# Two interleaved attention layers: the norm's statistics on ScalarE in two passes, its small steps on GpSimd, the pad in a tile of its own, and orders searched for it

## The chip, the cores and the metric

The kernel runs on one core of a Trainium2 chip. The metric is the device time of one execution in microseconds (us), taken as the median of several runs. A profiled execution of the same program gives the trace from which all other times here come. Engines are named as in the profile: PE is TensorE (matmul), PEld its weight load, DVE is VectorE, ACT is ScalarE, POOL is GpSimd, and SP is the engine whose queue starts the DMA transfers.

## What is computed

Four layers over 2048 tokens of width 512, each a residual around a norm and an attention of 32 heads of width 16. Layers 0 and 2 (type A) let each token attend to 8 tokens, 2 apart; layers 1 and 3 (type B) to the last 256 tokens. All numbers are float32 in and out.

```python
def _layernorm(x, axis=-1, eps=1e-5):
    m = jnp.mean(x, axis=axis, keepdims=True)
    v = jnp.var(x, axis=axis, keepdims=True)
    return (x - m) / jnp.sqrt(v + eps)
...
    x = A_x
    x = x + _A_ref(_layernorm(x, axis=-1), A_wqkv, A_wo)
    x = x + _B_ref(_layernorm(x, axis=-1), B_wqkv, B_wo)
    x = x + _A_ref(_layernorm(x, axis=-1), A_wqkv, A_wo)
    x = x + _B_ref(_layernorm(x, axis=-1), B_wqkv, B_wo)
    return x
```

## The kernel before, in words

The tokens are cut into 8 chunks of 256 (`C`), a chunk into two halves of 128 (`t` = 0, 1). For each chunk `layer_a` and then `layer_b` are recorded; layers 0 and 1 go over all chunks, then layers 2 and 3. That gives 32 norms, 16 ahead of A layers and 16 ahead of B layers.

**The norm** (`norm`, from L921). For each half DVE takes `bn_stats` (L936, 128x512) and `bn_aggr` (L939), which leave mean and variance in `mv`. Then come three small steps on 128x2 for both halves at once: `spread_` (L942, DVE) adds eps and scales, `rstd` (L945, POOL) raises to the power -1/2, `shift` (L948, DVE) multiplies the negative mean by that. With these two columns in `rs`, ACT normalises each half in one pass (L964 or L986). In a B layer, PE then transposes the result (L990), ACT copies it out as float16 high parts (L995) and DVE makes the low parts (L996); in an A layer a DMA transposes both parts. Projections (L1015 to L1017, and L1035 to L1038) follow on PE.

**An A layer.** DVE multiplies keys and queries (L1152), PE sums over heads (L1160), DVE and ACT make the softmax of 8 weights, PE spreads the weights (L1229), DVE weighs the values (L1242), and POOL (or DVE, L1247) sums them in three additions (L1249 to L1251).

**A B layer.** Queries and keys go through DRAM into the stacked tiles `stk` (L1286, L1297). A first pass of scores on PE (L1339, L1342) gives the maximum of each row on DVE: for most chunks a masked pick (L1361) and a reduction (L1357); in the first chunk of each B layer, which has no chunk before it, one instruction that adds a mask and takes the maximum (L1353). That instruction also writes its whole sum out, though only the maximum is used: the output goes to `junk`, a tile that nobody reads. The maxima join the stacked tiles as two more rows, so a second pass of scores (L1433, L1435) comes out with the maximum taken off; ACT takes the exponential (L1439), POOL sets the masked triangle to zero (L1448), and PE multiplies by the values (L1465).

**The residual** (`finish`). ACT (L1059) and POOL or DVE (L1061) split the attention's output into high and low parts, PE projects, and DVE adds the residual (L1069) into the tile `y` (or `x`), which the next norm reads.

**The pad.** Rows 48 to 63 and 112 to 127 of `stk` must hold zeros and two rows of a constant. POOL fills a small tile `pad` (L1556, L1558), first for `stk` 0, then for 1 and 2, and SP copies it out by 12 transfers (L1565). `pad` and `junk` come from the same one-buffer pool under the same tag, so they share one piece of memory.

**The order.** Nothing is scheduled at run time. `Plan.add` records every step with an engine and assumed times; `ORDER` gives each step a place in its engine's queue, and a negative place sends it to a second engine that is named at the step (`alt`). `Plan.order` then runs through the queues with those assumed times, only to settle which buffer and which PSUM banks each step gets. Semaphore waits between engines follow from the tiles that the steps touch. So an instruction that waits holds up all that stands behind it on its engine.

Of the kernel before, what the change touches and what calls it, by code (L numbers as in the profile page):

```python
# [18 lines left out]
P = 128  # L19
S = 2048  # L20
# [658 lines left out]
def kernel(  # L679
# [35 lines left out]
    ones = cst.tile([4, P], F32, name="ones")  # L715
    nc.gpsimd.memset(ones, 1.0)
    mhalf = cst.tile([P, 2], F32, name="mhalf")
    nc.gpsimd.memset(mhalf, -0.5)


    stk, vst = {}, {}
# [895 lines left out]
```

## Time and profile before

| what | value |
| --- | --- |
| median of 3 runs | 1440.65 us (1439.27 to 1445.52) |
| the profiled execution | 1440.79 us |
| its span, first to last instruction | 1439.1 us |
| ACT busy in the profiled execution | 736.9 us, 1058 instructions |
| POOL busy | 675.0 us, 769 instructions |

The span is the time between the first and the last instruction that the profiler recorded; 1.7 us of the execution lie around it. An engine's busy time is the union of its instructions' times. A row of the groups view reads: line, engine, operation, output and inputs by the program's tile names, shapes, count, then the busy time in us, the mean of one in ns, and after the bar the idle time of that engine just before these instructions, with what ended it. A row of the timeline reads: start, duration, engine and line, operation, tiles, and in brackets the engine's idle time before it and what ended that. Matmuls overlap in time, and their ends are modelled, so a busy PE is not PE at its peak.

### The profile page before, as it was taken

What the parts mean: (1) busy time and instruction counts of PE and PEld (TensorE: products, weight loads), DVE (VectorE), ACT (ScalarE), POOL (GpSimd) and SP (SyncE); (2) the same over time, 40 slices, a digit from 0 to 9 for tenths busy, and PEclk for the clock granted to TensorE, in tenths of its full rate; (3) what the DMA queues carried; (4) which work ended last, traced back from release to release, by engine and by line L of the source; (5) the groups of instructions that cost most, each with busy time, mean ns of one, the idle gap of its engine ahead of it and who ended that gap; (6) DMA issues with size and microseconds to landing.
All of it is one profiled execution on the core that took longest, in us unless ns stands there. A gap on an engine that the chain in (4) does not pass through costs nothing.

```text
span 1439.1 us, 35171 instructions
## 1 busy us (share of the span) xinstructions
PE 1339.7 (93%) x13918; PEld 783.0 (54%) x13918; DVE 1172.9 (82%) x2265; ACT 736.9 (51%) x1058; POOL 675.0 (47%) x769
## 2 busy tenths in 40 slices
PE   9975999999999999999999898998999999999997
PEld 7642646556364564647556363654637455464654
DVE  7877696997969879698996869798797978969694
ACT  6621445555555455455545444454555555545564
POOL 3425172552836337372562717355281643717343
PEclk9995989999999999999999999999999999999999
DMA  8241234233243333323233242323334143232332
GB/s 241 75 116 46 68 86 127 61 91 97 69 121 75 86 80 88 105 69 101 73 80 113 66 127 70 105 60 89 106 81 123 40 115 91 72 98 77 105 72 61
DMA packets 135943, 130.45 MB, mean 91 GB/s; under 512 B 68448, under 2 KB 94560, under 8 KB 135776
## 3 DMA queue, kind: packets, MB, share of 16 engines
q1 hardware_dynamic: 135520, 127.93, 33.1%
q8 instruction: 109, 1.79, 0.5%
q14 instruction: 58, 0.48, 0.1%
q10 hardware_dynamic: 256, 0.26, 0.1%
HBM read 67.11 MB, written 43.48 MB: 77 GB/s over the span
## 4 chain that ended last, share of the span: by engine, by line
PE 53%; DVE 19%; POOL 8%; issue 6%; DMA 5%; ACT 4%; SPq 4%; DVEq 0%; POOLq 0%; ACTq 0%
PE banks L1015 8%; PE banks L1017 7%; PE banks L1016 7%; PE banks L1465 6%; DVE m L1357 4%; PE banks L1037 3%; PE banks L1433 3%; POOL pw L1249 3%; PE banks L1160 3%; DVE banks L1361 3%; PE banks L1035 3%; PE banks L1038 3%; DVE pw L1242 3%; PE banks L1339 3%; ACT p L1439 2%
## 5 line engine op out<-in xcount | busy, mean ns | idle before, releaser
L1439 ACT ACTIVATE p<-banks,sclB 128x768 f32<-128x768 f32 x480 | 418.0, 901 | 289.1 <-PE banks L1435 204.7
L1448 POOL TENSOR_SCALAR_AFFINE_SELECT p<-p 128x1024 f32<-128x1024 f32 x240 | 262.9, 1104 | 368.2 <-ACT p L1439 286.0
L1357 DVE TENSOR_REDUCE m<-banks 128x2 f32<-128x512 f32 x448 | 296.6, 684 | 3.5
L1361 DVE COPY_PREDICATED banks<-maskt,banks 128x256 f32<-128x256 int16 x448 | 179.4, 421 | 72.2 <-PE banks L1342 65.3
L1465 PE MATMUL banks<-p,v 128*32 128x128 f32 (+1 forms) x3840 | 197.6, 333 | 5.6 <-POOL p L1448 3.3
L1152 DVE TENSOR_TENSOR pr<-kv,q 128x512 f32<-128x512 f32 x235 | 156.5, 716 | 24.4 <-PE banks L1160 18.3
L1433 PE MATMUL banks<-stk,stk 64*128 64x256 f16 x960 | 133.7, 284 | 28.7 <-ACT p L1439 9.3
L1465 PEld LDWEIGHTS banks<-p,v 128*32 128x32 f32 x3840 | 106.3, 110 | 96.9 <-issue 32.8
L1242 DVE TENSOR_TENSOR pw<-banks,kv 128x1024 f32<-128x1024 f32 x128 | 153.0, 1212 | 4.1 <-POOL o L1251 2.3
L1342 PE MATMUL banks<-stk,stk 48*128 48x128 f16 (+1 forms) x1024 | 128.8, 250 | 13.9 <-DVE m L1353 10.3
L1249 POOL TENSOR_TENSOR pw<-pw 128x512 f32<-128x512 f32 x100 | 127.4, 1274 | 22.8 <-DVE pw L1242 22.5
L1339 PE MATMUL banks<-stk,stk 48*128 48x128 f16 (+1 forms) x896 | 113.3, 252 | 17.3 <-DVE m L1357 5.9
L1433 PEld LDWEIGHTS <-stk 64*128 64x128 f16 x960 | 56.9, 95 | 121.7 <-issue 113.2
L1435 PE MATMUL banks<-stk,stk 64*128 64x128 f16 x960 | 108.0, 223 | 0.0
L1339 PEld LDWEIGHTS <-stk 48*128 48x128 f16 x896 | 50.2, 94 | 95.3 <-issue 86.7
L1276 DVE SCALAR_TENSOR_TENSOR el<-banks,eh 128x512 f16<-128x512 f32 x64 | 42.4, 684 | 72.8 <-DMA re<-eh 36.7
L1250 POOL TENSOR_TENSOR pw<-pw 128x256 f32<-128x256 f32 x100 | 72.9, 729 | 7.8
L1015 PE MATMUL banks<-xh,wA0h 128*128 128x256 f16 x256 | 70.1, 274 | 2.3 <-ACT p L1439 2.3
L1015 PE MATMUL banks<-xh,wA1h 128*128 128x256 f16 x256 | 71.3, 278 | 0.7 <-DVE pw L1242 0.7
L1017 PE MATMUL banks<-xh,wA1l 128*128 128x256 f16 x256 | 71.1, 278 | 0.0
L1016 PE MATMUL banks<-xl,wA1h 128*128 128x256 f16 x256 | 71.1, 278 | 0.0
L1342 PEld LDWEIGHTS <-stk 48*128 48x128 f16 x1024 | 53.0, 96 | 33.1 <-issue 31.1
(193 smaller groups left out, 3051.6 us busy)
## 6 DMA issues: line engine op xcount, KB each, us to landing
stk<-re SPq DMA_DIRECT2D x256, 96.0 KB
re<-eh SPq DMA_DIRECT2D x128, 128.0 KB
xm<-y SPq DMA_DIRECT2D x32, 256.0 KB
re<-el SPq DMA_DIRECT2D x64, 128.0 KB
y<-xm SPq DMA_DIRECT2D x32, 256.0 KB
oc<-os SPq DMA_DIRECT2D x120, 64.0 KB
os<-scr SPq DMA_DIRECT2D x15, 512.0 KB
x<-in_A_x_dram SPq DMA_DIRECT2D x16, 256.0 KB
```

The source lines that it names most:

```text
L1015: nc.tensor.matmul(ps[mp].t[:, i], wh, xh, start=k == 0, stop=False)
L1016: nc.tensor.matmul(ps[mp].t[:, i], wh, xl, start=False, stop=False)
L1017: nc.tensor.matmul(ps[mp].t[:, i], wl, xh, start=False, stop=k == 3)
L1242: nc.vector.tensor_mul(pw.t, pb.t.unsqueeze(1).broadcast_to([P, 2, W, 64]), v)
L1339: nc.tensor.matmul(ps.t[:, par, 0 : (2 - qb) * P], lhs, stk[hf, bef][r, col, qb * P :], start=True, stop=True)
L1342: nc.tensor.matmul(ps.t[:, par, (2 - qb) * P : 3 * P], lhs, stk[hf, now][r, col, : (1 + qb) * P], start=True, stop=True)
L1357: nc.vector.tensor_reduce(out=m.t[:, :, u, qb], in_=ps.t[:, :, 0 : 2 * P], op=ALU.max, axis=AX.X)
L1361: nc.vector.copy_predicated(t[:, :, 0:P], maskt[:, 0:P].bitcast(I16).unsqueeze(1).broadcast_to([P, 2, P]), t[:, :, 2 * P : 3 * P])
L1433: nc.tensor.matmul(o[:, two], k[:, jf * P : (jf + 1) * P], q, start=True, stop=True)
L1439: nc.scalar.activation(pt.t[:, :, 2 * i : 2 * i + 2].rearrange("p s m q -> p m s q"), ps.t[:, :, : 3 * P].rearrange("p m (s q) -> p m s q" ...
L1448: nc.gpsimd.affine_select(out=v, in_=v, pattern=[[0, 8], [-1 if b == 0 else 1, P]], compare_op=ALU.is_gt if b == 0 else ALU.is_ge, fill=0. ...
L1465: nc.tensor.matmul(o, v[:, jj, 17 * h : 17 * h + 32], rhs, start=z == 0 and (b == 0 or first), stop=z == 1 and b == 1, tile_position=(0, 3 ...
```

## The change

The two statistics of a half are now two ACT passes over the same 128x512. The first (`mean`) multiplies by -1/512 and sums, so `mv` gets the negative mean; the second (`squares`) adds that to the data and sums the squares, so `mv` gets 512 times the variance. Each pass writes its elementwise result to a new tile `unread`. `spread_` and `shift` go from DVE to POOL, next to `rstd`, with constants changed to fit. `bn_stats`, `bn_aggr` and the tile `b6` are gone. `unread` also takes the place of `junk` behind the masked maximum, and `pad` moves to the tag `rc`, whose buffer otherwise holds the softmax sums of B layers. All places in `ORDER` are new. The numbers of the diff's table say nothing by themselves, so only a line of it stands here.

```diff
 ORDER = {
-    "S": [0, 1, 4, 7],
...
+    unread = cst.tile([P, D], BF16, name="unread")
...
-        b6 = buf("psm", [P, 2, 6], F32, "b6", f"b6{l}_{c}")
         vmv, vr0, vrs = [Val(mv), Val(mv)], [Val(rs), Val(rs)], Val(rs)
-        vb6 = [Val(b6), Val(b6)]
+        vmean = [Val(mv), Val(mv)]
...
-        def stats(t):
-            nc.vector.bn_stats(b6.t[:, t], xs[t][0].t)
-
-        def aggr(t):
-            nc.vector.bn_aggr(mv.t[:, t], b6.t[:, t])
+        def mean(t):
+            nc.scalar.activation(unread, xs[t][0].t, AF.Identity, scale=-1.0 / D, accum_out=mv.t[:, 0, t : t + 1])
+
+        def squares(t):
+            nc.scalar.activation(unread, xs[t][0].t, AF.Square, bias=mv.t[:, 0, t : t + 1], accum_out=mv.t[:, 1, t : t + 1])
 
         def spread_():
-            nc.vector.tensor_scalar(rs.t[:, 0], mv.t[:, :, 1], 1.0e-5, 1.0 / (XS * XS), op0=ALU.add, op1=ALU.mult)
+            nc.gpsimd.tensor_scalar(rs.t[:, 0], mv.t[:, 1], D * 1.0e-5, 1.0 / (D * XS * XS), op0=ALU.add, op1=ALU.mult)
...
         def shift():
-            nc.vector.scalar_tensor_tensor(rs.t[:, 1], mv.t[:, :, 0], -1.0, rs.t[:, 0], op0=ALU.mult, op1=ALU.mult)
+            nc.gpsimd.tensor_tensor(out=rs.t[:, 1], in0=mv.t[:, 0], in1=rs.t[:, 0], op=ALU.mult)
 
         for t in range(2):
-            plan.add("DVE", 0.61, lambda t=t: stats(t), r=[xs[t][1]], w=[vb6[t]])
-            plan.add("DVE", 0.11, lambda t=t: aggr(t), r=[vb6[t]], w=[vmv[t]])
-        plan.add("DVE", 0.075, spread_, r=vmv, w=[vr0[0]])
+            plan.add("ACT", 0.72, lambda t=t: mean(t), r=[xs[t][1]], w=[vmean[t]])
+            plan.add("ACT", 0.9, lambda t=t: squares(t), r=[xs[t][1], vmean[t]], w=[vmv[t]])
+        plan.add("POOL", 0.25, spread_, r=vmv, w=[vr0[0]])
         plan.add("POOL", 0.72, rstd, r=[vr0[0]], w=[vr0[1]])
-        plan.add("DVE", 0.08, shift, r=[vr0[1], *vmv], w=[vrs])
+        plan.add("POOL", 0.3, shift, r=[vr0[1], *vmean], w=[vrs])
...
-                            junk = pools["ps1"][0].tile([P, 3 * P], BF16, tag="junk", name=f"j{l}_{c}")
...
-                                    out=junk[:, x0:], in0=ps.t[:, par, x0 : 3 * P], in1=maskt[:, x0:], scale=1.0, scalar=NEG,
+                                    out=unread[:, x0 : 3 * P], in0=ps.t[:, par, x0 : 3 * P], in1=maskt[:, x0:], scale=1.0, scalar=NEG,
...
-        pad = buf("ps1", [P, 3 * P], BF16, "junk", f"pad{some[0]}")
+        pad = buf("ps1", [P, 2, 64], F32, "rc", f"pad{some[0]}")
```

In the changed file the lines from L1353 on stand one lower (the masked maximum is L1352, the pick L1360, the reduction L1356, the exponential L1438, the triangle L1447), and L936 and L939 are the two ACT passes.

What the new places do to the queues is shown at two points. The first is on DVE, at the first masked maximum of the first B chunk; `j` in the old rows is the tile `junk`, and the names in brackets are the semaphores that an instruction waits for (DMAHW are those of transfers). Before:

```order
L1183 TENSOR_REDUCE mx_1_1349<-banks 128x64 [waits PE_49]
L1186 TENSOR_TENSOR e_1_1351<-banks,mx_1_1349 128x512 [waits DVE_49]
L1353 ISA j_0_1359,m_0_0_1360<-banks,maskt 128x256 [waits DMAHW5_49,DMAHW4_49,DMAHW6_49,DMAHW1_49,DMAHW7_49,DMAHW0_49,PE_49]
L1353 ISA m_0_0_1360 128x1
L1353 ISA j_0_1359,m_0_0_1360<-banks,maskt 128x256 [waits DVE_49,PE_49]
```

And with the change:

```order
L1183 TENSOR_REDUCE mx_1_1346<-banks 128x64 [waits PE_49]
L1186 TENSOR_TENSOR e_1_1350<-banks,mx_1_1346 128x512 [waits DVE_49]
L1352 ISA unread,m_0_0_1358<-banks,maskt 128x256 [waits PE_49]
L1352 ISA m_0_0_1358 128x1
L1352 ISA unread,m_0_0_1358<-banks,maskt 128x256 [waits DVE_49,PE_49]
```

The neighbours are the same; the instruction that waited on six semaphores of transfers and on PE now waits on PE alone.

The second point is the norm ahead of the B layer in chunk 4 of layer 1, from the residual `y` of the second half to the normalising passes. Before, on DVE:

```order
L1069 SCALAR_TENSOR_TENSOR y_4_1_3965<-banks,sclA_141,y_4_1_3965 128x512
L1061 TENSOR_TENSOR ol_2_4887<-oc_2_4577,oh_2_4874 128x4x128
L936 BN_STATS b_4_4842<-y_4_1_3965 128x6
L939 BN_AGGR mv_4_4867<-b_4_4842 128x2
L942 TENSOR_SCALAR rs_4_4905<-mv_4_4867 128x2
L1357 TENSOR_REDUCE m_3_2_4792<-banks 128x2
L1361 COPY_PREDICATED banks<-maskt,banks 128x2x128
L948 SCALAR_TENSOR_TENSOR rs_4_4905<-mv_4_4867,rs_4_4905 128x2
```

With the change these steps stand on ACT,

```order
L936 ACTIVATE unread,mv_4_4798<-y_4_0_4616 128x512
L1438 ACTIVATE p_3_1_1_4807<-banks,sclB_152 128x2x3x128
L939 ACTIVATE unread,mv_4_4798<-y_4_0_4616,mv_4_4798 128x512
L1438 ACTIVATE p_3_1_1_4807<-banks,sclB_152 128x2x3x128
L1059 CAST oh_2_4844<-oc_2_4516 128x4x128 x2
L936 ACTIVATE unread,mv_4_4798<-y_4_1_3805 128x512
L939 ACTIVATE unread,mv_4_4798<-y_4_1_3805,mv_4_4798 128x512
L1438 ACTIVATE p_3_2_0_4878<-banks,sclB_152 128x2x3x128
L986 ACTIVATE xn_4_0_4896<-y_4_0_4616,rs_4_4880 128x512
L1438 ACTIVATE p_3_2_1_4905<-banks,sclB_152 128x2x3x128
L986 ACTIVATE xn_4_1_4915<-y_4_1_3805,rs_4_4880 128x512
```

and on POOL:

```order
L1447 AFFINE_SELECT p_3_1_1_4807<-p_3_1_1_4807 128x1024
L942 TENSOR_SCALAR rs_4_4880<-mv_4_4798 128x2
L945 TENSOR_TENSOR rs_4_4880<-rs_4_4880,mhalf 128x2
L948 TENSOR_TENSOR rs_4_4880<-mv_4_4798,rs_4_4880 128x2
L942 TENSOR_SCALAR rs_5_4977<-mv_5_3918 128x2
```

The statistics of the second half are now the last ACT work ahead of the normalising passes, with one exponential between them and another between the two passes; the three small steps stand together on POOL, behind a triangle mask and ahead of those of the next norm.

Counted over all queues, DVE has 170 instructions fewer, ACT 115 and POOL 60 more (the profile further counts the reading of each of ACT's 128 sums as an instruction); PE and SP have as many as before. Beside the norm's steps these changed their engine: 11 low parts (L1061) and 4 divisions of B's output (L1540) went from POOL to DVE, 10 key-query products (L1152) from DVE to POOL, 5 sums of squares of the weights (L830 and L832) from ACT to DVE, and a few steps of a quarter of a microsecond or one single step of their kind.

More of the change, by code (lines that the diff above doesn't have):

```diff
@@ L1548, with zeros @@
     prep("B")
+    def zeros(pad):
+        return pad.t.rearrange("p a b -> p (a b)").bitcast(F16)
     for some in ((0,), (1, 2)):
-        pad = buf("ps1", [P, 3 * P], BF16, "junk", f"pad{some[0]}")
+        pad = buf("ps1", [P, 2, 64], F32, "rc", f"pad{some[0]}")
         vpad = Val(pad)
         def fill(some=some, pad=pad):
-            v = pad.t.bitcast(F16)
+            v = zeros(pad)
             nc.gpsimd.memset(v[0:16, 0:C], 0.0)
@@ L1564, in put @@
                     for par in range(2):
-                        nc.sync.dma_start(stk[hf, i][64 * par + 48 : 64 * par + 64], pad.t.bitcast(F16)[0:16, 0:C].unsqueeze(1).broadcast_to([16, 8, C]))
+                        nc.sync.dma_start(stk[hf, i][64 * par + 48 : 64 * par + 64], zeros(pad)[0:16, 0:C].unsqueeze(1).broadcast_to([16, 8, C]))
                 plan.add("SP", 1.3, put, r=[vpad],
```

837 rows, old and new, of the table ORDER are left out of this document.

## The prediction

> **What bounds the kernel now.** I read the page first, then a table by stages.
>
> ```profile
> span 1439.1 us, 35171 instructions
> PE 1339.7 (93%) x13918; PEld 783.0 (54%) x13918; DVE 1172.9 (82%) x2265; ACT 736.9 (51%) x1058; POOL 675.0 (47%) x769
> PE 53%; DVE 19%; POOL 8%; issue 6%; DMA 5%; ACT 4%; SPq 4%; DVEq 0%; POOLq 0%; ACTq 0%
> ```
>
> The third line is the chain of waits: PE carries half of it, DVE a fifth. But the averages hide two stages that alternate, as four stretches of 45 us from the middle show (engine, busy us, instructions):
>
> ```profile
> 990.00:1035.00 45.00, 44.31 (x492) 30.80 (x493) 33.26 (x68) 22.44 (x34) 12.61 (x13) 1.00 0.34 95
> 1035.00:1080.00 45.00, 41.35 (x447) 18.87 (x440) 43.39 (x73) 24.89 (x35) 32.30 (x37) 1.00 0.33 85
> 1080.00:1125.00 45.00, 44.11 (x488) 30.39 (x488) 33.34 (x65) 23.02 (x34) 8.43 (x10) 1.00 0.43 113
> 1125.00:1170.00 45.00, 42.15 (x445) 19.28 (x442) 43.34 (x75) 25.25 (x36) 33.49 (x39) 0.92 0.27 74
> ```
>
> The columns after the length are PE, PEld, DVE, ACT, POOL, then PE's granted clock. In the first and third stretch PE is full (44 of 45) and DVE has a quarter free; in the second and fourth DVE is full (43.4 of 45), PE loads a third fewer weights per us (18.9 against 30.8), and its busy time there is partly waiting. So a microsecond taken from DVE is worth up to a microsecond in one half of the program and little in the other. ACT has nearly half of each stretch free.
>
> **What is taken from DVE.** The groups view gives the norm's steps:
>
> ```profile
> L936 DVE BATCH_NORM_STATS2 b<-x 128x6 f32<-128x512 f32 x32 | 21.8, 683 | 6.9 <-DMA x<-in_A_x_dram 6.4 <-DMA x<-xd 0.2
> L936 DVE BATCH_NORM_STATS2 b<-y 128x6 f32<-128x512 f32 x32 | 21.7, 683 | 0.1
> L939 DVE BATCH_NORM_AGGREGATE mv<-b 128x2 f32<-128x6 f32 x64 | 10.7, 173 | 0.3
> L942 DVE TENSOR_SCALAR rs<-mv 128x2 f32<-128x2 f32 x32 | 7.3, 228 | 0.7
> L948 DVE SCALAR_TENSOR_TENSOR rs<-mv,rs 128x2 f32<-128x2 f32 x32 | 17.6, 548 | 4.2 <-POOL rs L945 4.1
> ```
>
> 21.8 + 21.7 + 10.7 + 7.3 + 17.6 = 79.1 us leave DVE. The new order gives some back. The prices:
>
> ```profile
> L1061 POOL TENSOR_TENSOR ol<-oc,oh 128x512 f16<-128x512 f32 x24 | 27.8, 1162 | 22.8 <-ACT oh L1059 22.8
> L1061 DVE TENSOR_TENSOR ol<-oc,oh 128x512 f16<-128x512 f32 x8 | 5.4, 682 | 3.8 <-DMA y<-xm 3.8
> L1540 POOL TENSOR_TENSOR oc<-oc,os 128x512 f32<-128x512 f32 x12 | 15.2, 1268 | 1.8 <-DMA os<-scr 1.5 <-issue 0.2
> L1540 DVE TENSOR_TENSOR oc<-oc,os 128x512 f32<-128x512 f32 x18 | 13.0, 750 | 0.7 <-DMA os<-scr 0.7
> L1152 POOL TENSOR_TENSOR pr<-kv,q 128x512 f32<-128x512 f32 x21 | 25.5, 1224 | 60.6 <-PE banks L1160 42.0 <-ACT q L1131 16.0 <-ACT kv L1133 2.7
> L1152 DVE TENSOR_TENSOR pr<-kv,q 128x512 f32<-128x512 f32 x235 | 156.5, 716 | 24.4 <-PE banks L1160 18.3 <-ACT kv L1133 2.9 <-ACT q L1131 2.8
> L832 DVE CUSTOM_DVE_ANT_0 wA0l<-stk 128x1024 bf16<-128x1024 f32 x2 | 2.6, 1300 | 0.9 <-DMA stk<-in_A_wqkv_dram 0.8
> ```
>
> On DVE: 11 low parts x 0.682 + 4 divisions x 0.750 - 10 products x 0.716 + 5 sums of squares x 1.300 = +9.8 us. DVE ends about 79.1 - 9.8 = 69 us lighter. What is a microsecond of it worth? Low: the chain holds 19% of 1439.1 = 273 us of DVE's 1172.9 busy us, so 0.23. High: the full stretches are half of the program, so 0.5. I take 0.35, between them, since the steps ahead of a B layer lie at the end of the full stretches. 69 x 0.35 = **-24 us** (bounds -16 to -35).
>
> **What ACT gets.** No sum of a 128x512 is in the trace, but its parts are:
>
> ```profile
> L974 ACT CAST ht<-xn 128x512 f16<-128x512 f32 x30 | 17.8, 613 | 1.9 <-DMA xh<-ht 1.5
> L1212 ACT ACTIVATE e<-e,sclA 128x512 f32<-128x512 f32 x16 | 11.5, 721 | 16.2 <-DVE e L1186 16.1
> L830 ACT ACTIVATION_READ_ACCUMULATOR wB1l<-stk 128x1 f32 x2 | 0.4, 187 | 0.0
> L986 ACT ACTIVATE xn<-y,rs 128x512 f32<-128x512 f32 x32 | 24.4, 807 | 38.9 <-DVE rs L948 37.6 <-PE banks L990 1.3
> ```
>
> The first pass is like the cast, which reads no factor from a tile (0.613), the second like the exponential, which reads one (0.721); each has a sum read out (0.187). That is 64 x 0.80 + 64 x 0.91 = 109 us; a second pass as dear as L986 (0.807), which reads two, would make it 115. Five sums of squares leave ACT (about 6 us), so **+103 us** of work on ACT. Little of it is on the path: ACT stood idle for 38.9 us right before L986, waiting for the very steps that it now does itself. By the chain, 4% of 1439.1 = 58 of ACT's 737 busy us count, 0.08 each, so **+8 us** (0 if the idle time takes all of it).
>
> **What POOL gets.** The nearest rows to a POOL step on 128x2 are a small copy and the power itself:
>
> ```profile
> L1123 POOL COPY kv<-ha 128x56 f32<-128x56 f32 x28 | 7.4, 265 | 58.8 <-DVE pr L1152 58.6
> L945 POOL TENSOR_TENSOR rs<-rs,mhalf 128x2 f32<-128x2 f32 x32 | 24.4, 764 | 68.1 <-DVE rs L942 57.6 <-PE banks L1342 6.7 <-DVE rs L948 3.0
> ```
>
> I take 0.27 for each, by the copy: nothing but the power needs a long formula. 64 x 0.27 = 17 us, at most 64 x 0.76 = 49. With -11 x 1.162 - 4 x 1.268 + 10 x 1.224 = -5.6 for the steps that moved, POOL ends 12 us busier (up to 43). POOL holds 8% of the chain, 115 of 675 us, 0.17 each: **+2 us** (up to +7).
>
> **The path of one norm.** Layer 1, chunk 4, from the last residual to the normalising pass:
>
> ```profile
> 562.04 0.74 DVE L1069 SCALAR_TENSOR_TENSOR y<-banks,sclA,y 128x512 f32<-128x512 f32 x1
> 562.82 0.69 DVE L936 BATCH_NORM_STATS2 b<-y 128x6 f32<-128x512 f32 x1
> 563.75 0.17 DVE L939 BATCH_NORM_AGGREGATE mv<-b 128x2 f32<-128x6 f32 x1
> 563.96 0.17 DVE L942 TENSOR_SCALAR rs<-mv 128x2 f32<-128x2 f32 x1
> 564.21 0.71 POOL L945 TENSOR_TENSOR rs<-rs,mhalf 128x2 f32<-128x2 f32 x1 [0.48 <-DVE rs L942]
> 564.88 1.15 POOL L1061 TENSOR_TENSOR ol<-oc,oh 128x512 f16<-128x512 f32 x1
> 565.10 0.95 DVE L948 SCALAR_TENSOR_TENSOR rs<-mv,rs 128x2 f32<-128x2 f32 x1
> 566.09 1.52 ACT L986 ACTIVATE xn<-y,rs 128x512 f32<-128x512 f32 x2 [2.47 <-DVE rs L948]
> ```
>
> From 562.78 to 566.09 are 3.3 us. The new path is 0.80 + 0.91 on ACT, 0.27 + 0.71 + 0.27 on POOL and four hand-overs of 0.08 (as from L942's end at 564.13 to L945 at 564.21): 3.3 us. So the path stays as long, and the pair of ACT passes fits in the 2.47 us for which ACT stood idle; I charge nothing. Behind the waiting passes on ACT stand exponentials, for which POOL's mask and then PE wait.
>
> Note L948: 0.95 us for two columns, and it ends with POOL's L1061, which began before it. The Trainium skill (SBUF — State Buffer, "Who interferes with whom") says that a DVE instruction with two SBUF inputs and a GpSimd instruction that reads SBUF exclude each other for their whole length; the row agrees. By that rule the moved `shift` and `spread_` can in turn be held up by DVE's two-input steps; the sum already allows for it with its upper POOL price.
>
> **The pad.** One wait at the first masked maximum, with the queue that it waits for:
>
> ```profile
> 105.86 0.44 PE L1342 MATMUL banks<-stk,stk 48*128 48x256 f16 x5 [0.53 <-DMA stk<-re]
> 108.76 1.31 SPq L1565 DMA_DIRECT2D stk<-pad  x2
> 112.14 0.42 DVE L1353 CUSTOM_DVE_ANT_0 j<-banks,maskt 128x256 bf16<-128x256 f32 x1 [6.12 <-DMA stk<-pad]
> 112.62 0.26 PE L1342 MATMUL banks<-stk,stk 48*128 48x128 f16 x1 [6.32 <-DVE m L1353]
> ```
>
> DVE wants to write `junk`, but the transfers from `pad`, in the same memory, have not been read out; PE then waits for DVE. With `unread` apart the scores at 106 are all that DVE needs. The next limit is SP, which issues the stacked tiles in turn until about 112.6; the first group of scores does not need the last of them. I take **-5 us** (bounds 0 and -6.3). It is a wait that falls away once; layers 2 and 3 fill no pad.
>
> **Sum.** 1440.8 (the profiled execution, 0.1 from the median) - 24 + 8 + 2 - 5 = **1422 us**. With each term at its own bounds and nothing else, 1440.8 - 35 + 0 + 1 - 6 = 1401 to 1440.8 - 16 + 8 + 7 - 0 = 1440.
>
> **Rivals.** (1) *The norm's path becomes longer, and PE waits for it; slower.* Place: the 16 norms ahead of B layers. In front of the last pair on ACT or between the normalising passes stands an exponential (0.9 us by L1439), in front of the POOL steps a mask (1.1 by L1448):
>
> ```profile
> L1439 ACT ACTIVATE p<-banks,sclB 128x768 f32<-128x768 f32 x480 | 418.0, 901 | 289.1 <-PE banks L1435 204.7 <-PE banks L1465 48.2 <-DVE m L1357 14.6
> L1448 POOL TENSOR_SCALAR_AFFINE_SELECT p<-p 128x1024 f32<-128x1024 f32 x240 | 262.9, 1104 | 368.2 <-ACT p L1439 286.0 <-issue 57.4 <-ACT mt L1381 8.5
> L990 PE MATMUL banks<-idf,xn 128*128 128x128 f32 x136 | 21.7, 287 | 10.3 <-ACT xn L986 9.1 <-DVE m L1357 1.2
> ```
>
> If both come late, the path grows by 2.0 us, 16 x 2.0 = +32 us, if PE has no other projection to run meanwhile: 1422 + 32 = 1454. It comes out slower than before from 1.2 us per norm on (19 / 16). For it: these queues are in order, and ACT and POOL now both stand in a row on the path. Against: PE waits only 10.3 us in all before the transposes, the last row, and the steps that DVE ran between the norm's are no longer in it. (2) *Nothing but the pad.* PE is the bound and DVE's lightening only makes it wait for PE: 1440.8 - 5 = 1436. For it: 53% of the chain. Against: the full DVE stretches. (3) *All goes well:* half of DVE's 69 us paid in full and ACT's work free: 1401. (4) *The moved small steps do not count.* In a sentence that the rest can do without: the Trainium skill (Perfetto Trace Analysis, "Optimizing Scalar/DVE Operations") warns that moving work between GpSimd and DVE might not help, as they share a read port. As a mechanism here: DVE loses L942 and L948, 24.9 us, but stands blocked as long elsewhere, so 44 us x 0.35 = -15, and 1440.8 - 15 + 8 + 2 - 5 = 1431. The L948 rows show the blocking, but with POOL's 1.15 us steps, not with short ones.
>
> **Chances.** Forecast 0.44 (own range 1408 to 1437), rival 1 0.22, rival 2 0.10, rival 3 0.20, rival 4 0.04. A difference of under 0.5% (7.2 us) could not be told from no change: faster means below 1433.4, slower above 1447.9. Faster: 0.41 of the forecast, all of rival 3, 0.03 of rival 4: 0.64. Slower: rival 1, 0.22. Same: the rest, 0.14. The range 1396 to 1455 leaves out the far halves of rivals 1 and 3.
>
> **What the changed profile would show.** DVE busy near 1104 us, ACT near 840, POOL near 687; ACT's passes at 0.61 and 0.72 with a read of 0.19; no wait of 6 us at the first masked maximum; the idle time before L986 well below 38.9; PE's busy time less than before by nearly the gain. The forecast is wrong if PE's waits for transposes (L990) grow beyond 15 us, or if the DVE-full stretches stay as long with DVE less than full in them: then something else set their length, POOL above all.

## The result and the profile after

| kernel | median | runs | ratio to before, 95% interval |
| --- | --- | --- | --- |
| before | 1443.09 us (1439.27 to 1445.93) | 4 | |
| changed | 1428.37 us (1426.56 to 1432.05) | 4 | 0.9914 [0.9889, 0.9938] |

The change makes the kernel faster by 0.9%; the forecast was 1422. The profiled execution took 1428.45 us, 12.3 less than the 1440.79 of before. The page of the changed kernel, the lines that answer to the first three of the prediction:

```profile
span 1426.7 us, 35354 instructions
PE 1340.1 (94%) x13918; PEld 788.4 (55%) x13918; DVE 1127.4 (79%) x2095; ACT 817.5 (57%) x1296; POOL 689.6 (48%) x829
PE 64%; DVE 13%; POOL 7%; ACT 5%; issue 5%; DMA 4%; SPq 3%; ACTq 0%; POOLq 0%; DVEq 0%
```

DVE is 45.5 us less busy, ACT 80.6 more, POOL 14.6 more. In the chain of waits PE rose from 53 to 64% and DVE fell from 19 to 13%: the kernel now waits less for DVE and more for PE itself.

The norm's groups, and two that the new order sends to DVE more often:

```profile
L936 ACT ACTIVATE unread<-y 128x512 bf16<-128x512 f32 x32 | 20.0, 626 | 21.8 <-DVE y L1069 17.8 <-DVE m L1352 4.0
L936 ACT ACTIVATION_READ_ACCUMULATOR unread<-y 128x1 f32 x32 | 6.0, 189 | 0.0
L939 ACT ACTIVATE unread<-y,mv 128x512 bf16<-128x512 f32 x32 | 23.1, 720 | 4.0 <-DVE m L1352 3.2
L942 POOL TENSOR_SCALAR rs<-mv 128x2 f32<-128x2 f32 x32 | 11.9, 373 | 67.0 <-ACT unread L939 66.4
L945 POOL TENSOR_TENSOR rs<-rs,mhalf 128x2 f32<-128x2 f32 x32 | 24.2, 758 | 2.7
L948 POOL TENSOR_TENSOR rs<-mv,rs 128x2 f32<-128x2 f32 x32 | 7.5, 233 | 2.4
L986 ACT ACTIVATE xn<-y,rs 128x512 f32<-128x512 f32 x32 | 24.6, 808 | 17.4 <-POOL rs L948 16.1 <-PE banks L990 1.3
L990 PE MATMUL banks<-idf,xn 128*128 128x128 f32 x136 | 21.9, 299 | 4.1 <-ACT xn L986 4.1
L1061 DVE TENSOR_TENSOR ol<-oc,oh 128x512 f16<-128x512 f32 x20 | 14.5, 738 | 4.1 <-ACT oh L1059 3.9
L1539 DVE TENSOR_TENSOR oc<-oc,os 128x512 f32<-128x512 f32 x22 | 19.5, 903 | 1.5 <-DMA stk<-md 0.9 <-DMA os<-scr 0.6
```

The two passes and the read of their sum last what the forecast took from the rows of other ACT instructions. ACT's idle time before the normalising pass (L986) fell from 38.9 to 17.4 us, PE's before the transposes (L990) from 10.3 to 4.1. New is an entry that no forecast had: both passes wait for `m` of L1352, the masked maximum of the first chunks, with which they have no number in common.

The norm whose rows the prediction shows, now in the timeline of the changed kernel, from the last residual to the normalising pass. By its place among the norms it is that of chunk 6 of layer 1, and not of chunk 4, as the prediction calls it:

```profile
561.10 0.74 DVE L1069 SCALAR_TENSOR_TENSOR y<-banks,sclA,y 128x512 f32<-128x512 f32 x1
562.11 0.62 ACT L936 ACTIVATE unread<-y 128x512 bf16<-128x512 f32 x1
562.62 0.19 ACT L936 ACTIVATION_READ_ACCUMULATOR unread<-y 128x1 f32 x1
562.85 0.72 ACT L939 ACTIVATE unread<-y,mv 128x512 bf16<-128x512 f32 x1
563.86 0.19 POOL L942 TENSOR_SCALAR rs<-mv 128x2 f32<-128x2 f32 x1
564.13 0.71 POOL L945 TENSOR_TENSOR rs<-rs,mhalf 128x2 f32<-128x2 f32 x1
564.92 0.20 POOL L948 TENSOR_TENSOR rs<-mv,rs 128x2 f32<-128x2 f32 x1
565.15 1.52 ACT L986 ACTIVATE xn<-y,rs 128x512 f32<-128x512 f32 x2 [0.98 <-POOL rs L948]
```

From 561.84 to 565.15 are 3.3 us, as before and as forecast. But this norm is a lucky pick: in chunk 4 the same path went from 2.8 to 3.7 us, and on the mean of the 16 norms ahead of B layers from 3.33 to 3.71. What changed in the norm shown is that DVE is not in it any more, and that POOL's long step (L1061), which held `shift` up for 0.95 us on DVE, now stands behind it on the same engine.

Where the time came from can be followed by the first normalising pass ahead of each B chunk. Counted from each span's start, the changed kernel is 5.7 us late at the first (84.8 against 79.1), level at the sixth (482.7, 482.6), and 11.8 ahead at the last (1323.5, 1335.3). So it loses at the start and then gains about 1.2 us a chunk on the mean. Three questions follow: what the norm's move is worth and what the orders are, what became of the pad's 5 us, and what the shared `unread` costs.

### The profile page after: what moved, and what is told of

Same layout as the page of the kernel before. It is cut to its first block, busy times and chain, and to the rows that moved or that the text cites. A ratio compares the mean times of both kernels' runs of the same rounds, so it can differ in the third digit from the quotient of the medians.

```text
span 1426.7 us, 35354 instructions
## 1 busy us (share of the span) xinstructions
PE 1340.1 (94%) x13918; PEld 788.4 (55%) x13918; DVE 1127.4 (79%) x2095; ACT 817.5 (57%) x1296; POOL 689.6 (48%) x829
## 4 chain that ended last, share of the span: by engine, by line
PE 64%; DVE 13%; POOL 7%; ACT 5%; issue 5%; DMA 4%; SPq 3%; ACTq 0%; POOLq 0%; DVEq 0%
PE banks L1015 10%; PE banks L1016 8%; PE banks L1017 8%; PE banks L1464 8%; PE banks L1037 4%; PE banks L1035 4%; PE banks L1432 4%; PE banks L1038 4%; PE banks L1160 4%; DVE pw L1242 3%; PE banks L1339 3%; DVE m L1356 3%; ACT p L1438 2%; POOL pw L1249 2%; PE banks L1342 2%
## 5 line engine op out<-in xcount | busy, mean ns | idle before, releaser
L1438 ACT ACTIVATE p<-banks,sclB 128x768 f32<-128x768 f32 x480 | 417.6, 899 | 241.5 <-PE banks L1434 194.8
L1447 POOL TENSOR_SCALAR_AFFINE_SELECT p<-p 128x1024 f32<-128x1024 f32 x240 | 262.4, 1101 | 334.6 <-ACT p L1438 325.2
L1356 DVE TENSOR_REDUCE m<-banks 128x2 f32<-128x512 f32 x448 | 297.6, 687 | 4.1
L1360 DVE COPY_PREDICATED banks<-maskt,banks 128x256 f32<-128x256 int16 x448 | 179.0, 424 | 80.8 <-PE banks L1342 79.6
L1152 DVE TENSOR_TENSOR pr<-kv,q 128x512 f32<-128x512 f32 x225 | 152.8, 731 | 37.2 <-PE banks L1160 21.5
L1342 PE MATMUL banks<-stk,stk 48*128 48x128 f16 (+1 forms) x1024 | 130.8, 253 | 11.2 <-DVE m L1352 7.9
L1249 POOL TENSOR_TENSOR pw<-pw 128x512 f32<-128x512 f32 x100 | 127.2, 1272 | 12.8 <-DVE pw L1242 12.7
L1339 PE MATMUL banks<-stk,stk 48*128 48x128 f16 (+1 forms) x896 | 114.2, 254 | 19.4 <-DVE m L1356 6.5
L1276 DVE SCALAR_TENSOR_TENSOR el<-banks,eh 128x512 f16<-128x512 f32 x64 | 42.6, 686 | 79.6 <-ACT eh L1273 52.6
L1015 PE MATMUL banks<-xh,wA1h 128*128 128x256 f16 x256 | 70.9, 277 | 1.0 <-ACT wA1h L912 1.0
L1015 PE MATMUL banks<-xh,wB1h 128*128 128x256 f16 x256 | 71.2, 278 | 0.7 <-ACT xh L995 0.7
L1017 PE MATMUL banks<-xh,wA1l 128*128 128x256 f16 x256 | 70.8, 277 | 0.9 <-DVE wA1l L910 0.9
L1016 PE MATMUL banks<-xl,wB1h 128*128 128x256 f16 x256 | 70.9, 277 | 0.4 <-DVE xl L996 0.4
```

What stands on the lines that cost most here:

```text
L1015: nc.tensor.matmul(ps[mp].t[:, i], wh, xh, start=k == 0, stop=False)
L1016: nc.tensor.matmul(ps[mp].t[:, i], wh, xl, start=False, stop=False)
L1017: nc.tensor.matmul(ps[mp].t[:, i], wl, xh, start=False, stop=k == 3)
L1339: nc.tensor.matmul(ps.t[:, par, 0 : (2 - qb) * P], lhs, stk[hf, bef][r, col, qb * P :], start=True, stop=True)
L1342: nc.tensor.matmul(ps.t[:, par, (2 - qb) * P : 3 * P], lhs, stk[hf, now][r, col, : (1 + qb) * P], start=True, stop=True)
L1356: nc.vector.tensor_reduce(out=m.t[:, :, u, qb], in_=ps.t[:, :, 0 : 2 * P], op=ALU.max, axis=AX.X)
```

## The experiments

Before's own median was 1440.3 to 1441.6 us beside these runs and 1443.1 beside the changed kernel's, so a difference between kernels that were measured at different times is uncertain by 2 to 3 us. Where a kernel moves a step "in its body", the step keeps its place in the recorded order and only the instruction that it issues belongs to another engine; it stands in that engine's queue where the order has it.

### The pad alone, in the old order: b_apart

```diff
-  junk = pools["ps1"][0].tile([P, 3 * P], BF16, tag="junk", name=f"j{l}_{c}")
+  junk = pools["ps1"][0].tile([P, 3 * P], BF16, tag="max", name=f"j{l}_{c}")
```

> The kernel before with one edit: the unread output of the masked maximum has memory of its own, apart from the pad. Norm, orders and everything else are as before. If the 6.1 us wait of DVE (and 6.3 us of PE) at the first masked maximum set the length there, the time falls by 5 to 6 us, to about 1438, and that wait is gone. If SP's queue of stacked tiles or a later wait sets it, the wait is gone but the time stays within 2 us of before.

Measured: 1434.82, ratio 0.9958 [0.9941, 0.9976]. The first masked maximum starts at 106.0 us where it stood at 112.1, without a wait:

```profile
106.04 0.41 DVE L1353 CUSTOM_DVE_ANT_0 j<-banks,maskt 128x256 bf16<-128x256 f32 x1
```

The lead of 6 us is kept to the end (6.2 us at the second norm ahead of a B layer, 6.6 at the end): under the old order the whole of the wait is paid out.

### The norm's move in the old order: b_move, b_move2

In b_move the norm's steps and the pad are those of the change, while the order is that of before. b_move2 also takes the masked maximum away from `unread` (it writes over its own scores), so that ACT and DVE share no tile:

```diff
-  nc.vector.bn_stats(b6.t[:, t], xs[t][0].t)
+  nc.scalar.activation(unread, xs[t][0].t, AF.Identity, scale=-1.0 / D, accum_out=mv.t[:, 0, t : t + 1])
-  nc.vector.bn_aggr(mv.t[:, t], b6.t[:, t])
+  nc.scalar.activation(unread, xs[t][0].t, AF.Square, bias=mv.t[:, 0, t : t + 1], accum_out=mv.t[:, 1, t : t + 1])
...
-  out=junk[:, x0:], in0=ps.t[:, par, x0 : 3 * P]                  # before
+  out=unread[:, x0 : 3 * P], in0=ps.t[:, par, x0 : 3 * P]         # b_move
+  out=ps.t[:, par, x0 : 3 * P], in0=ps.t[:, par, x0 : 3 * P]      # b_move2
```

> The whole change (norm on ACT and POOL, unread tile, pad apart) but in the orders of before: each moved step stands on its new engine where its planned moment in the old order puts it. If the lighter DVE itself brings the gain (0.35 us for each of its 79 us, less 10 for ACT and POOL), this run shows most of it: 1422 to 1432. If the gain comes from the new orders, the old ones fit the moved steps badly and it is no faster than before: 1438 or more.

> The kernel before with its own orders, the norms' bodies on ScalarE and GpSimd as in b_move, and the masked maximum written over its own scores, so that VectorE and ScalarE share no unread tile. b_move took 1466.0. If the tile that both engines write and nobody reads costs the same 10 us here as under the changed orders, about 1456, still slower than before by some 1%, and PE's transposes still wait over 20 us for ScalarE's xn. The rival, that most of b_move's loss was the shared tile and not the longer path of the norm: 1440 to 1447, with those waits near the 10 us of before. If the sharing costs nothing under these orders: 1466.

Measured: b_move 1466.0, ratio 1.0172 [1.0151, 1.0194]; b_move2 1462.38, ratio 1.0147 [1.012, 1.0173]. Both are slower than before, though DVE is 60 us less busy. Two groups of b_move2 (lines stand one lower than before):

```profile
PE 1342.3 (92%) x13918; PEld 782.2 (54%) x13918; DVE 1112.0 (76%) x2073; ACT 823.9 (56%) x1314; POOL 687.9 (47%) x833
L991 PE MATMUL banks<-idf,xn 128*128 128x128 f32 x136 | 23.5, 299 | 27.6 <-ACT xn L987 27.4
L987 ACT ACTIVATE xn<-y,rs 128x512 f32<-128x512 f32 x32 | 24.4, 807 | 31.0 <-POOL rs L949 29.7 <-PE banks L991 1.3
```

PE now waits 27.6 us before the transposes, against 10.3 before and 10.6 in b_apart (pad apart, old order, norm on DVE):

```profile
L990 PE MATMUL banks<-idf,xn 128*128 128x128 f32 x136 | 21.7, 287 | 10.6 <-ACT xn L986 9.4 <-DVE m L1357 1.2
```

This is the mechanism of the slower rival. From the last residual to the first normalising pass the 16 norms ahead of B layers take 3.39 us on the mean in b_apart and 4.49 in b_move2. That is 1.1 us more for each, 17.6 in all, and PE's wait before the transposes grew by 17.0. The rival had 2.0 us for each and 32 in all. The kernel as a whole lost 1462.4 - 1434.8 = 27.6 us (the same figure as the wait's total by chance); where the other 10 us of it went is not shown. The shared tile explains only the 4 us between b_move and b_move2, and their intervals overlap.

### The new order with the norm back on DVE: a_dve

```diff
-  nc.scalar.activation(unread, xs[t][0].t, AF.Identity, scale=-1.0 / D, accum_out=mv.t[:, 0, t : t + 1])
+  nc.vector.bn_stats(b6[:, t], xs[t][0].t)
-  nc.scalar.activation(unread, xs[t][0].t, AF.Square, bias=mv.t[:, 0, t : t + 1], accum_out=mv.t[:, 1, t : t + 1])
+  nc.vector.bn_aggr(mv.t[:, t], b6[:, t])
...
-  nc.gpsimd.tensor_tensor(out=rs.t[:, 1], in0=mv.t[:, 0], in1=rs.t[:, 0], op=ALU.mult)
+  nc.vector.scalar_tensor_tensor(rs.t[:, 1], mv.t[:, :, 0], -1.0, rs.t[:, 0], op0=ALU.mult, op1=ALU.mult)
```

> The changed kernel with its own orders, but the statistics and the two small steps back on DVE (mean and variance by the two batch-norm instructions); pad and unread tile stay apart. If a microsecond of DVE is worth 0.35, its 79 us cost 24 to 28 us less what ACT and POOL give back (10): 1440 to 1450. If the new orders carry the gain by themselves, it stays at 1426 to 1432.

Measured: 1455.33, ratio 1.009 [1.0069, 1.0111]. The new order without the move is slower than before too. In this kernel only DVE writes `unread`, so it has no shared tile.

### The shared tile: a_two, a_junk

In the change ACT's passes and the masked maximum write the same `unread`. Two ways to part them, one in PSUM and one in SBUF:

```diff
-  out=unread[:, x0 : 3 * P], in0=ps.t[:, par, x0 : 3 * P]
+  out=ps.t[:, par, x0 : 3 * P], in0=ps.t[:, par, x0 : 3 * P]      # a_two
...
+  junk = pools["ps1"][0].tile([P, 2 * P], BF16, tag="junk", name=f"j{l}_{c}")
+  out=junk[:, 0 : 3 * P - x0], in0=ps.t[:, par, x0 : 3 * P]       # a_junk
```

> The changed kernel with one edit: the masked maximum of the first B chunks writes its unread output over its own scores in PSUM, not into the tile that ACT's passes write too. So DVE and ACT no longer wait for each other over a tile that nobody reads (5.9 us of DVE and 9.4 us of ACT waits in the changed profile). If those waits are on the path, the time falls by 3 to 6 us; if they are covered, it stays within 1.5 us of the changed kernel.

> The changed kernel with a buffer of its own in SBUF for the masked maximum's unread output; the pads stay in rc and ScalarE keeps its unread tile. Only the sharing of the tile goes away, and the output stays in SBUF (a_two wrote it to PSUM). If the sharing was what cost 10 us in the changed kernel, 1417 to 1420, as a_two. If a_two's gain came from writing to PSUM, so that SBUF had one writer fewer, 1427 to 1429, as the changed kernel.

Measured: a_two 1418.62, ratio 0.985 [0.9826, 0.9874]; a_junk 1421.49, ratio 0.9876 [0.9847, 0.9905]. So the sharing cost the changed kernel 5 to 7 us: 6.9 by the medians (1428.4 - 1421.5), 5.5 by the ratios to before, whose intervals overlap by a little, though the slowest run of a_junk (1424.4) is faster than the fastest of the changed kernel (1426.6). Whether the output in PSUM brings 3 more is not settled, as the intervals of these two overlap. The view of waits of the changed kernel shows the mechanism (engine and line, what it waited for, us in all, times, longest):

```profile
ACT unread L936 <- DVE m L1352: 6.2, 4, 2.7
DVE unread L1352 <- ACT unread L939: 3.5, 3, 1.8
ACT unread L939 <- DVE m L1352: 3.2, 3, 1.6
DVE unread L1352 <- ACT unread L936: 2.4, 3, 0.8
```

Nobody reads `unread`, but two engines write it, and each write waits until the one before it, on the other engine, has ended. It happens in the first chunk of each B layer, where masked maxima and norms alternate. From the first masked maximum to the last, the changed kernel takes 64.8 us in layer 1 and 61.8 in layer 3; a_junk takes 61.9 and 58.3, which is 6.4 us of the 6.9. More of these stretches lies at half of PE's clock in the changed kernel's trace (30.7 and 10.2 us against 27.3 and 3.4), so it is not shown that the waits alone make the 6.4.

### The pad in the new order: a_pad

```diff
+  junk = pools["ps1"][0].tile([P, 2 * P], BF16, tag="junk", name=f"j{l}_{c}")
-  out=unread[:, x0 : 3 * P], in0=ps.t[:, par, x0 : 3 * P]
+  out=junk[:, 0 : 3 * P - x0], in0=ps.t[:, par, x0 : 3 * P]
...
-  pad = buf("ps1", [P, 2, 64], F32, "rc", f"pad{some[0]}")
+  pad = buf("ps1", [P, 2 * P], BF16, "junk", f"pad{some[0]}")
```

> The changed kernel with the pad's part undone: the pads and the masked maximum's output share one buffer again (of 512 B a partition), as in the kernel before, so the first masked maximum waits for the pad's last transfer; ScalarE's unread tile is its own, so the false sharing of the changed kernel is gone too, as in a_two (1418.6). In the changed kernel the last pad transfer is issued at 116.1 us and the first masked maximum starts at 113.9. If the pad's part is worth its wait under the changed orders as it was under the old ones (6 us), the first masked maximum starts near 119 and the time is 1422 to 1425. The rival, that the late start of the changed kernel covers the wait and the pad's part is worth nothing here: 1417 to 1420, with the first masked maximum near 115.

Measured: 1429.1, ratio 0.9928 [0.9905, 0.9952], 7.6 us above a_junk, from which it differs in the pad alone. The first masked maximum, in the timeline of the changed kernel with SP's last pad transfers, and after that in a_pad:

```profile
113.27 0.69 DVE L1186 TENSOR_TENSOR e<-banks,mx 128x512 f32<-128x512 f32 x1
113.88 0.41 DVE L1352 CUSTOM_DVE_ANT_0 unread<-banks,maskt 128x256 bf16<-128x256 f32 x1
115.45 1.30 SPq L1567 DMA_DIRECT2D stk<-pad  x2
```

```profile
113.64 0.69 DVE L1186 TENSOR_TENSOR e<-banks,mx 128x512 f32<-128x512 f32 x1
119.05 0.42 DVE L1353 CUSTOM_DVE_ANT_0 j<-banks,maskt 128x256 bf16<-128x256 f32 x1 [4.72 <-DMA stk<-pad]
```

The new order issues the last pad transfers at 115.45 us (before: 108.76), so the late start does not cover the wait: with the shared buffer it is there again, 4.72 us.

### A late start by ACT's statistics? a_head

Here the norms of chunks 1 to 3 of layer 0 have DVE's statistics and small steps again; all else is the changed kernel.

```diff
+  on_dve = (l, c) in ((0, 1), (0, 2), (0, 3))
...
+  if on_dve:
+      nc.vector.bn_stats(b6[:, t], xs[t][0].t)
+      return
```

> The changed kernel with the norms of chunks 1 to 3 of the first layer back on DVE, which ACT has to do while it prepares the weights; all else and the orders unchanged. If ACT's statistics delay the weights, the first norm ahead of a B layer comes 3 to 5 us earlier than its 84.8 us and the end follows by most of that: 1423 to 1426. If the late start comes from the new order of loads or of SP's queue, nothing moves by more than 1.5 us, or DVE gets in the way and it is slower.

Measured: 1427.36, ratio 0.991, and the first normalising pass ahead of a B chunk at 85.3 us. Nothing: the 5.7 us at the start are not the price of these passes. In a_dve, where all statistics are on DVE under the new order, that pass stands at 87.5. But b_move2, under the old order, has it at 86.6 where b_apart has it at 78.9. So either part of the change by itself brings a late start, and why was not tested; the order of the weights' preparation is one candidate.

### The small steps back on DVE: a_small

```diff
-  nc.gpsimd.tensor_scalar(rs.t[:, 0], mv.t[:, 1], D * 1.0e-5, 1.0 / (D * XS * XS), op0=ALU.add, op1=ALU.mult)
+  nc.vector.tensor_scalar(rs.t[:, 0], mv.t[:, 1], D * 1.0e-5, 1.0 / (D * XS * XS), op0=ALU.add, op1=ALU.mult)
-  nc.gpsimd.tensor_tensor(out=rs.t[:, 1], in0=mv.t[:, 0], in1=rs.t[:, 0], op=ALU.mult)
+  nc.vector.tensor_tensor(out=rs.t[:, 1], in0=mv.t[:, 0], in1=rs.t[:, 0], op=ALU.mult)
```

> The changed kernel with the two small steps of each norm back on DVE at their planned moments, the statistics still on ACT. If POOL is the right place, DVE pays 7 us for the first and 18 us for the second (which waits for POOL's long steps) at 0.35 each, +5 to +9 us. If the three steps in a row on POOL are what holds the path, it is faster by 3 us or more; if both are covered, within 1.5 us of the changed kernel.

Measured: 1436.95, ratio 0.9976 [0.9958, 0.9994], 8.6 us above the changed kernel. The groups of a_small:

```profile
L942 DVE TENSOR_SCALAR rs<-mv 128x2 f32<-128x2 f32 x32 | 5.8, 181 | 0.8 <-ACT unread L939 0.7
L948 DVE TENSOR_TENSOR rs<-mv,rs 128x2 f32<-128x2 f32 x32 | 10.8, 337 | 5.8 <-POOL rs L945 5.7
L986 ACT ACTIVATE xn<-y,rs 128x512 f32<-128x512 f32 x32 | 24.6, 808 | 27.5 <-DVE rs L948 26.3 <-PE banks L990 1.3
```

DVE gets 16.6 us of steps and 5.8 us of standing before L948, and ACT stands 10 us longer before the normalising pass. The places were made for the steps on POOL, so a part of the 8.6 us may be the price of the misfit.

### The price of work: b_twice, a_twice, a_sums

b_twice issues `bn_stats` twice in the kernel before; a_twice issues the first ACT pass twice in the changed one.

```diff
   nc.vector.bn_stats(b6.t[:, t], xs[t][0].t)
+  nc.vector.bn_stats(b6.t[:, t], xs[t][0].t)                                                               # b_twice
...
   nc.scalar.activation(unread, xs[t][0].t, AF.Identity, scale=-1.0 / D, accum_out=mv.t[:, 0, t : t + 1])
+  nc.scalar.activation(unread, xs[t][0].t, AF.Identity, scale=-1.0 / D, accum_out=mv.t[:, 0, t : t + 1])   # a_twice
```

> The kernel before with each of the 64 batch-norm statistics on DVE issued twice, same output: 43.5 us more of DVE at the places of the norms and nothing else. It measures what a microsecond of DVE is worth there: +10 us at 0.23 (the chain's share), +15 at 0.35 (the forecast's value), +22 at 0.5 (the full stretches).

> The changed kernel with the first of the two ACT passes issued twice in each of the 64 statistics, same output: 64 x 0.82 = 52 us more of ACT at the norms. If ACT's time there lies beside other work as the forecast has it (0.08 for each us), +4 us. If the passes stand on the path of the 16 norms ahead of B layers, the second half's pass counts in full there: +13 us or more.

Measured: b_twice 1475.62, ratio 1.0238 [1.0218, 1.0258], that is +34 for 43.7 us of DVE, 0.78 per us. a_twice 1448.85, ratio 1.006 [1.0037, 1.0083], +20.5 for 52 us of ACT, 0.39 per us; DVE's waits for `unread` grew by 3.8 us in it, so some of that price is the shared tile's.

a_sums starts from a_two and takes ACT's first pass away in layers 1 to 3, where DVE's residual gives the sum of the row on the way:

```diff
-  nc.vector.scalar_tensor_tensor(xb.t, ps.t, scl[T, 3], xb.t, op0=ALU.mult, op1=ALU.add)
+  nc.vector.scalar_tensor_tensor(xb.t, ps.t, scl[T, 3], xb.t, op0=ALU.mult, op1=ALU.add, accum_out=sums[c][:, t : t + 1])
...
+  if given:   # l > 0; mean(t) then issues nothing
+      nc.scalar.activation(unread, xs[t][0].t, AF.Square, scale=-1.0 * D, bias=dsum[:, t : t + 1], accum_out=mv.t[:, 1, t : t + 1])
...
+      nc.gpsimd.tensor_scalar(mv.t[:, 0], dsum, -1.0 / D, 0.0, op0=ALU.mult, op1=ALU.add)
+      nc.gpsimd.tensor_scalar(rs.t[:, 0], mv.t[:, 1], D ** 3 * 1.0e-5, 1.0 / (D ** 3 * XS * XS), op0=ALU.add, op1=ALU.mult)
```

> The changed kernel with the masked maximum written over its own scores (as in a_two) and without ScalarE's first pass in the norms of layers 1 to 3: the residual's VectorE instruction that makes the rows also gives their sums (accum_out), ScalarE squares 512 x minus the sum, and GpSimd turns the sum into the mean's negative in one more small step beside that pass. Layer 0's norms keep both passes, and all orders stay the changed kernel's. ScalarE loses 48 passes of 0.63 + 0.19 us, 39 us; GpSimd gets 24 small steps of some 0.25 us, VectorE nothing unless the accumulator costs it time (then up to 0.1 us x 64). If ScalarE's work costs the 0.39 us per us that the doubled pass showed, in both directions, the time falls by 15 from a_two's 1418.6 to about 1403 (1398 to 1409), ScalarE's busy time by about 39. The rival: the orders were laid out around the pass, so what falls away becomes idle time of ScalarE and the next wait ends where it did: 1414 to 1420. If the accumulator makes the residual slow, or sends the DVE instructions into waits, above 1422.

Measured: 1414.37, ratio 0.9817 [0.979, 0.9845], the fastest of all kernels here. But it is only 4 us below a_two, and the intervals overlap: the rival of that run was right. Its page and groups:

```profile
PE 1330.0 (94%) x13918; PEld 784.4 (56%) x13918; DVE 1124.2 (80%) x2159; ACT 785.2 (56%) x1200; POOL 698.9 (49%) x853
L1082 DVE DVE_READ_ACCUMULATOR y<-banks,sclA,y 128x1 f32 x32 | 2.6, 82 | 0.0
L999 ACT ACTIVATE xn<-y,rs 128x512 f32<-128x512 f32 x32 | 24.6, 808 | 20.3 <-POOL rs L961 19.0 <-PE banks L1003 1.3
```

ACT lost 32 us of busy time (817.1 in a_two) and stands idle instead. Taken away under an order that was laid out around it, ACT's work is worth some 4.3 / 39 = 0.11 per us, which these runs do not tell apart from nothing (and DVE's reads of the sums, 5.2 us, and 24 steps on POOL came in with it); added, 0.39. A doubled cost gives the price of more of it, and not that of less.

## Why the prediction was nearly right, point by point

**The total.** 1422 forecast, 1428.4 measured: faster, as said, by two thirds of the 19 us. Two slips in the prediction's working change nothing in its sum: PE loads two fifths fewer weights per us in the second stretch (18.9 against 30.8), not a third, and the +1 for POOL in the lower bound is not worked out. Four kernels without a shared tile and with the pad apart split the change into its two large parts:

| | old order | new order |
| --- | --- | --- |
| norm on DVE | 1434.8 (b_apart) | 1455.3 (a_dve) |
| norm on ACT and POOL | 1462.4 (b_move2) | 1421.5 (a_junk) |

Either part alone costs 20 to 28 us; both together gain 13.3. (b_move2 writes the masked maximum to PSUM; the kernel that does so under the new order is a_two, 1418.6, and with it the two gain 16.2.) The change is therefore not "the norm's move, and a better order": this order is what makes the move pay, and neither of the two has a gain of its own. Whether another order, searched with the norm left on DVE, would have gained as much was not tried. The forecast for the two together was -24 + 8 + 2 = -14. That it meets the 13.3 is in good part luck, as the factors below show; and the forecast nowhere says that the gain hangs on both parts being there.

**DVE, -24.** Right in sign, with both factors off. The relief: 45.5 us of busy time instead of 69. Summed over DVE's groups, the norm's steps took 79.6 us away, as counted, but 22.9 came back instead of 9.8: the low parts (L1061) and the divisions (L1539) together went from 20.0 to 34.7 us where the forecast had 10.5 more, and the products that left freed 3.9 us instead of 7.2. A division took 903 ns on the mean and not 750, since 6 of the 22 took 1.14 to 1.66 us. In each of these six a POOL step of over 1 us had begun at most 0.5 us earlier, in five of them the triangle mask; so at 306.9 us:

```profile
306.94 1.60 DVE L1539 TENSOR_TENSOR oc<-oc,os 128x512 f32<-128x512 f32 x1
306.90 1.09 POOL L1447 TENSOR_SCALAR_AFFINE_SELECT p<-p 128x1024 f32<-128x1024 f32 x1
```

The remaining 11.2 us overlapped other DVE instructions, so that busy time, a union, did not fall by them. The price: the forecast took 0.35, between DVE's share of the chain and the full stretches. Work added costs 0.78 per us by b_twice; the part of the span in which PE is not busy grew there from 99.4 to 127.2 us, and 9.7 us of that growth are its wait before the transposes, so the chain's share was no measure of it:

```profile
L991 PE MATMUL banks<-idf,xn 128*128 128x128 f32 x136 | 23.3, 299 | 20.0 <-ACT xn L987 17.4 <-DVE m L1358 2.4
```

What DVE work taken away brings was measured by no run. a_dve against a_junk gives (1455.3 - 1421.5) / (1174.0 - 1125.7) = 0.70 for each us of DVE's busy time, but ACT and POOL lose their new work in it too, and it stands under an order made for the other place. At 0.70 to 0.78, 45.5 us would be worth 32 to 35, not 24: a smaller relief at a higher price.

**ACT, +8.** The durations were right (0.613 and 0.721 forecast, 0.626 and 0.720 measured, 0.187 and 0.189 for the sum). So was the amount: summed over its instructions ACT has 101 us more, 103 forecast, of which some 20 overlap each other, so that busy time rose by 80.6. The price of 0.08 lies far below the 0.39 for work added, and is not told apart from the 0.11 for work taken away. How much of ACT's work the new order really hides was not measured by itself.

**POOL, +2.** `spread_` took 0.373 and `shift` 0.233, forecast 0.27 each; POOL is 689.6 busy, forecast 687. The mean of `spread_` is made by seven long ones of 32, which run beside DVE's steps (last section); the prediction's upper POOL price allowed for such. Rival 4, that the moved small steps do not count, has 44 us of relief and 1431, which is near the 45.5 and 1428.4 measured, but not its mechanism: only three DVE instructions that ran beside the norm's steps on POOL took over 15% longer than the median of their kind, 2.1 us in all, where the rival needs 24.9. And a_small loses 8.6 us by moving them back. The Trainium skill (Perfetto Trace Analysis, "Optimizing Scalar/DVE Operations") warns that moving work between these two engines might not help. By a_small it does here, as far as a run that also breaks the order can tell.

**The pad, -5.** Right in mechanism, a little small: 6 us in the old order, 7.6 in the new (6.7 in the traces, of which 4.7 are DVE's wait).

**What failed: the sentence "With `unread` apart the scores at 106 are all that DVE needs."** `unread` is apart from `pad`, but it is shared by ACT and DVE, and no term was charged for that. It costs 5 to 7 us, about what the pad's part brings: a_pad, which has neither, takes 1429.1, the changed kernel, which has both, 1428.4. Without it the forecast of 1422 is a_junk's 1421.5. (1434.8 after the pad, less 13.3, plus 6.9 is 1428.4, but so it must be, since the terms are differences of these same runs.)

**The granted clock.** No term of the forecast and none above has PE's clock, which is not the same in these kernels. On the mean of their runs it is 0.961 for before, beside b_apart's 0.965; 0.958 for the changed kernel and a_pad; 0.962 for a_junk and 0.963 for a_two. In the trace of before, the projections at L1015 to L1017 take 273 ns in the median where the clock is whole and 421 where it is halved. In the 50 runs of before that were made beside the experiments, a clock higher by 0.01 goes with a time shorter by some 8 us. So about 3 us of the pad's 6 to 8, and as much of the shared tile's 5 to 7, go with the clock. Whether the waits bring the lower clock about or something else does was not tested. The 20 to 34 us between the four kernels of the table are far beyond it.

**The slower rival** was real in its mechanism under the old order, at about half of its size (17 us of waits before the transposes, 32 forecast), and the new order took the waits away: 4.1 us, well below the 15 that would have refuted the forecast. It did so without making the path short again, which takes 3.71 us on the mean where it took 3.33 before. So the forecast's "I charge nothing" held for PE, though the path did not stay as long: under the new order PE waits less for a path that takes longer. The argument against it, that steps which DVE ran between the norm's are no longer on the path, does not hold by itself: they are gone from b_move2's path as well.

**The signs named ahead.** The wait at the masked maximum is gone, and ACT's idle time before L986 fell. DVE (1127.4, forecast 1104) and ACT (817.5, forecast 840) moved by less. PE's busy time did not fall (1340.1, before 1339.7), but it does once the tile is not shared (1332.7 in a_junk). That trace has the higher clock too (0.963 against 0.957), so what made the difference is not settled. The last sign, the four stretches of 45 us:

```profile
990.00:1035.00 45.00, 44.55 (x506) 30.52 (x506) 30.44 (x57) 26.01 (x42) 11.70 (x14) 1.00 0.36 105
1035.00:1080.00 45.00, 42.06 (x423) 19.98 (x424) 41.42 (x68) 29.46 (x50) 28.89 (x37) 1.00 0.28 77
1080.00:1125.00 45.00, 45.00 (x529) 29.86 (x526) 35.37 (x65) 31.52 (x52) 16.09 (x20) 1.00 0.38 105
1125.00:1170.00 45.00, 41.91 (x417) 21.51 (x416) 39.45 (x68) 24.18 (x40) 29.31 (x36) 0.92 0.34 83
```

In the second and fourth DVE has 41.4 and 39.5 us to do where it had 43.4; it is still the fullest engine beside PE there, but no longer full. As the changed kernel is some 7 us ahead by then, the same cuts hold other work. From the twelfth norm ahead of a B layer to the fourteenth, two whole turns, the time went from 171.2 to 169.9 us and DVE's busy time in it from 145.2 to 140.8. So the turns stayed nearly as long with a DVE that has less to do, which comes near the forecast's second sign of being wrong. What sets their length now was not tested; POOL, which the forecast named, is busy for 28.9 and 29.3 of the 45 us in these stretches.

## What to carry to other kernels

When work moves between engines in a kernel with a fixed order, try the four combinations of old and new place with old and new order: a single undone part measures a misfit, not the part's worth. An output that nobody reads is still a write, so give each engine its own place for it, or let it overwrite data that is dead on that engine. And price work by adding some of it only for the question what more of it would cost; what less of it brings can be several times smaller.

## What was not expected of the hardware

- A sum taken along in DVE's residual (a_sums) costs nothing in the instruction itself (744 to 745 ns with it, 744 to 746 in a_two without) and 82 ns for the read of the accumulator behind it; on ACT the same read takes 188 ns.
- POOL's step on 128x2 (L942) takes 0.19 us in 24 of 32 cases, as in the norm above, but 0.373 on the mean: seven took 0.42 to 2.59 us. In each of the seven a DVE instruction is running, and it ends 0.05 to 0.06 us before POOL's step does; so in chunk 4 of layer 1, where DVE ends at 397.26 and POOL at 397.31:

```profile
396.58 0.68 DVE L1061 TENSOR_TENSOR ol<-oc,oh 128x512 f16<-128x512 f32 x1
396.61 0.70 POOL L942 TENSOR_SCALAR rs<-mv 128x2 f32<-128x2 f32 x1 [1.42 <-ACT unread L939]
```
